# A list of 1371 steps in another order: linear-attention chunks, a weight fold and a multiplicative feed-forward block interleaved by one text

## The chip, the cores and the metric

The kernel runs on one core of one Trainium2 chip. Five engines work at once: TensorE (PE; its weight loads are listed apart as PEld), VectorE (DVE), ScalarE (ACT), GpSimd (POOL) and SyncE (SP), which here only issues transfers. The metric is the time of one execution in microseconds (us). The kernel before took 601.12 us, the median of three executions (600.37 to 601.99). A profile of one execution shows every instruction with its start, its length and what it waited for.

## The reference

Four batches of eight heads run a delta-rule recurrence over 768 positions with a head size of 48; the result, as 3072 tokens of 384 features, goes through a feed-forward block whose two input products are multiplied with each other.

```python
def _attn_ref(q, k, v, beta):                      # (4, 8, 768, 48), beta (4, 8, 768)
    k_n = k / (np.linalg.norm(k, axis=-1, keepdims=True) + 1e-06)
    state = np.zeros((B, H, D, D), dtype=np.float32)
    for t in range(S):
        kt, vt, bt = (k_n[:, :, t], v[:, :, t], beta[:, :, t, None])
        y[:, :, t] = np.einsum('bhd,bhde->bhe', q[:, :, t], state)
        v_old = np.einsum('bhde,bhd->bhe', state, kt)
        state = state + bt[:, :, :, None] * np.einsum('bhd,bhe->bhde', kt, vt - v_old)

def _moe_ref(x, w1, w2, w3, w_out):                # (3072, 384), 384x1024, 1024x1024, 1024x384
    a = x @ w1
    b = x @ w2
    h = a * b @ w3
    return h @ w_out
```

## The kernel before

The sequence is cut into 12 chunks m of 64 positions. Within a chunk the recurrence is a triangular system; two chunks together make one pair j (or u) of 128 positions, for which the triangular blocks are inverted at once. The weights w3 and w_out are multiplied into one 1024x384 matrix first (the fold), so that the feed-forward block needs two products with w1 and w2, their product element by element, and one more product. The last one is done with seven block products instead of eight, so sums of weight blocks and of activation blocks are formed on POOL. All weights are rounded on the way in: every 128-row piece goes through a raw buffer and is converted by two ACT passes (L717, L720), one DVE pass (L722) and one POOL pass (L724).

All of this is written as generators. A part is one generator, named by a letter and numbers; each time its name stands in ORDER, `step` runs it up to its next `yield`. So a step is the piece between two yields, mostly a few instructions of one engine. Below, X.n is the n-th time that X stands in the list, hence its n-th piece. After the list is through, `in_text_order` (L161) chains all instructions of each engine in the order in which they were written. Every engine, SP and ACT with their transfers among them, therefore executes in the order of the list and waits at the head of its own sequence; the list cannot change what is computed, only who comes first.

The parts, with the lines of their instructions:

- `k`m, `q`m, `v`m: load a chunk of k (L204, four transfers), q or v (L215, two). `k0` and `q0` are issued by ACT, all others by SP. `beta` loads and transposes beta (L961, L968, L973). `p`m loads a chunk in permuted form (L232, eight transfers for k, eight for q).
- `K`m, `Q`m (m below 4): transposes on TensorE (L339), copied out of PSUM by DVE and ACT (L351, L349). For the later chunks `d`m does this on DVE (L326).
- `g`j: squares on POOL (L272), row sums on DVE (L274), an exchange through TensorE (L257). `N`j: fifteen small DVE instructions for the norms (L281 to L305) and another exchange.
- `s`m: scores on TensorE (L369, L375), then DVE and ACT or POOL (L381, L393, L395, L399). `u`m stores the blocks to DRAM (L416).
- `V`j: loads the blocks (L428), inverts them with 31 pairs of DVE instructions (L442, L449) and stores them (L457). For the first two pairs, V0 and V1, the block lies in one of the two PSUM tiles of the kind `w`, which is held from the copies V.3 and V.4 (L436) to V.67 and V.68 (L453); until then the other parts that need such a tile share the one that is left.
- `e`m: loads the inverse (L466, L473), a DVE transpose (L485), two groups of small TensorE products (L502) with ACT copies (L518, L529) for the corner block.
- `n`m: v times the norm on POOL (L541). `c`m: the chain through the state, three groups of TensorE products of 64 passes or more (L555; c.1, c.3, c.5) with DVE after each (L588, L598, L617 or L619). `y`m: the outputs (L656, two groups with a drain between), ACT copies (L677), transfers within SBUF (L688).
- `P`i: loads a weight piece (L708): P0 to P3 w_out, P4 to P11 w3, P12 to P14 w1, P15 to P17 w2. `C`i: converts one half of a piece; piece i has C2i and C2i+1. There are three raw buffers, taken in turn, so a load waits for POOL to finish both halves of the piece three loads before.
- `t`i: transposes of w3 (L762, L765). `f`jc: the fold, two halves of four products with 384 columns (L771), then ACT (L778). f.1 needs C0 to C3, f.2 needs C4 to C7.
- `b`jc: chunk 0 of pair 0, and `a`ujc: the rest of pair u, in eight column blocks jc: product with w1 (L791), ACT copy (L803), product with w2 (L791), DVE multiplication (L807). Their PSUM tiles are four of the kind `f`, taken in turn.
- `T`: sums of weight blocks on POOL (L840). `S`u: sixteen sums of activation blocks on POOL (L860). `o`u: the seven block products (L888). `x`u: results on ACT and DVE (L919, L923, L925) and stores (L905).

TensorE's order therefore mixes long steps (a, b, o, f: four to sixteen products of 192 to 512 columns) with small ones (hundreds of matmul passes with 16 to 128 columns). The critical sequence at the start is: k and q in, K and Q, N0, s0 and s1, u0 and u1, V0, e0, c0, y0, c1, y1, and from there the products a and b. The fold and the transposes fill TensorE meanwhile.

Of the kernel before, what the change touches and what calls it, by code (L numbers as in the profile page):

```python
# [1064 lines left out]
```

## Time and profile before

| what | us |
|---|---|
| median of three executions | 601.12 |
| the profiled execution | 601.93 |
| its span, first to last instruction | 600.2 |
| TensorE busy | 542.4 |
| DVE / POOL / ACT busy | 329.7 / 173.6 / 164.2 |
| TensorE idle in 0 to 160 / 160 to 380 / 380 to 600 | 44.6 / 5.5 / 7.5 |
| mean granted TensorE clock, as a share of full speed | 0.98 |

Over the whole span TensorE is busy nine tenths of the time and no other engine more than 55%. In 40 slices (each digit the busy share of 15 us in tenths, 9 for 90% or more) the beginning differs from the rest:

```profile
PE   2378994889899999999999899999999999999997
DVE  2457763457786379665696644975545963211012
ACT  3486653734312211131211312012310111320100
POOL 6364433230535700207203016021071001500051
PEclk9988996899999999999999989999999999999999
DMA  8959887596953356525546352463253021010001
```

The DMA row is the mean busy share of the 16 transfer engines; it is high in the first eleven slices, in which all weights and the first chunks come in. The chain of waits, followed back from the last instruction, spends its time so:

```profile
PE 80%; DMA 6%; issue 4%; DVE 4%; ACT 4%; SPq 1%; POOL 0%; ACTq 0%; DVEq 0%
```

"issue" is time in which an engine waited for nothing that the profile shows. TensorE's own waits, longest in total first:

```profile
PE ps_f L339 <- DMA ktok<-in_k_dram: 11.0, 2, 9.2
PE ps_f L968 <- ACT KQ L349: 8.8, 1, 8.8
PE ps_w L502 <- issue: 7.8, 2, 6.1
PE ps_w L656 <- issue: 5.3, 5, 2.2
PE ps_w L375 <- issue: 4.7, 3, 2.2
PE ps_f L771 <- ACT w3T L765: 3.5, 2, 2.2
PE ps_f L791 <- POOL w2s L724: 2.8, 2, 2.3
```

A line names the engine, the tile and line that waited, what ended the wait, and then the sum in us, the number of waits and the longest.

### The profile page before, as it was taken

What the parts mean: (1) busy time and instruction counts of PE and PEld (TensorE: products, weight loads), DVE (VectorE), ACT (ScalarE), POOL (GpSimd) and SP (SyncE); (2) the same over time, 40 slices, a digit from 0 to 9 for tenths busy, and PEclk for the clock granted to TensorE, in tenths of its full rate; (3) what the DMA queues carried; (4) which work ended last, traced back from release to release, by engine and by line L of the source; (5) the groups of instructions that cost most, each with busy time, mean ns of one, the idle gap of its engine ahead of it and who ended that gap; (6) DMA issues with size and microseconds to landing.
All of it is one profiled execution on the core that took longest, in us unless ns stands there. A gap on an engine that the chain in (4) does not pass through costs nothing.

```text
span 600.2 us, 19394 instructions
## 1 busy us (share of the span) xinstructions
PE 542.4 (90%) x8444; PEld 378.7 (63%) x8444; DVE 329.7 (55%) x788; ACT 164.2 (27%) x345; POOL 173.6 (29%) x222
## 2 busy tenths in 40 slices
PE   2378994889899999999999899999999999999997
PEld 2364663658678884558854569645588446884477
DVE  2457763457786379665696644975545963211012
ACT  3486653734312211131211312012310111320100
POOL 6364433230535700207203016021071001500051
PEclk9988996899999999999999989999999999999999
DMA  8959887596953356525546352463253021010001
GB/s 225 219 135 276 233 163 128 82 176 96 164 80 55 56 123 108 98 42 84 103 78 127 50 81 73 82 114 65 40 86 94 14 59 32 5 54 13 1 0 53
DMA packets 204404, 56.54 MB, mean 94 GB/s; under 512 B 193344, under 2 KB 199488, under 8 KB 202528
## 3 DMA queue, kind: packets, MB, share of 16 engines
q1 hardware_dynamic: 200128, 54.52, 46.4%
q10 hardware_dynamic: 4192, 0.79, 0.9%
q8 instruction: 66, 1.08, 0.8%
q14 instruction: 18, 0.15, 0.1%
HBM read 43.09 MB, written 11.01 MB: 90 GB/s over the span
## 4 chain that ended last, share of the span: by engine, by line
PE 80%; DMA 6%; issue 4%; DVE 4%; ACT 4%; SPq 1%; POOL 0%; ACTq 0%; DVEq 0%
PE ps_f L791 39%; PE ps_f L888 18%; PE ps_w L555 5%; PE ps_f L771 5%; PE ps_w L656 4%; DMA raw<-in_moe_w_dram 3%; PE ps_w L502 3%; PE ps_w L369 2%; PE ps_w L375 2%; DMA ktok<-in_k_dram 2%; DVE ps_w L449 1%; DVE tb L442 1%; DMA Vd<-Vb 1%; ACT raw L720 1%; PE ps_w L888 1%
## 5 line engine op out<-in xcount | busy, mean ns | idle before, releaser
L791 PE MATMUL ps_f<-xT,w2s 128*128 128x512 f32 (+1 forms) x336 | 134.2, 544 | 3.0 <-POOL w2s L724 2.8
L860 POOL TENSOR_TENSOR ab<-ab 128x256 f32<-128x256 f32 x96 | 66.8, 728 | 223.5 <-DVE ab L807 190.0
L791 PE MATMUL ps_f<-xT,w1s 128*128 128x512 f32 (+1 forms) x336 | 128.2, 532 | 0.3 <-issue 0.3
L791 PEld LDWEIGHTS ps_f<-xT,w2s 128*128 128x128 f32 x336 | 62.5, 191 | 57.9 <-issue 50.9
L791 PEld LDWEIGHTS ps_f<-xT,w1s 128*128 128x128 f32 x336 | 63.3, 190 | 55.8 <-issue 51.7
L803 ACT COPY ab<-ps_f 128x512 f32<-128x512 f32 (+1 forms) x56 | 27.9, 527 | 185.6 <-PE ps_f L791 185.6
L888 PE MATMUL ps_f<-w,ab 128*128 128x192 f32 x376 | 66.3, 330 | 0.0
L807 DVE TENSOR_TENSOR ab<-ab,ps_f 128x512 f32<-128x512 f32 (+1 forms) x56 | 32.9, 604 | 59.1 <-PE ps_f L791 58.5
L888 PEld LDWEIGHTS ps_f<-w,ab 128*128 128x128 f32 x376 | 61.2, 190 | 3.9 <-issue 2.7
L442 DVE TENSOR_TENSOR tb<-Vb,Ub 128x31 f32<-128x31 f32 (+15 forms) x124 | 43.9, 354 | 16.4 <-DMA Ub<-Ud 13.0
L771 PE MATMUL ps_f<-w2s,w3T 128*128 128x384 f32 x128 | 45.4, 507 | 4.9 <-ACT w3T L765 3.5
L888 PE MATMUL ps_f<-room,ab 128*128 128x192 f32 x272 | 48.0, 330 | 0.8 <-DVE room L919 0.8
L449 DVE TENSOR_TENSOR Vb<-Vb,tb 128x31 f32<-128x31 f32 (+15 forms) x124 | 44.6, 360 | 4.3
L888 PEld LDWEIGHTS ps_f<-room,ab 128*128 128x128 f32 x272 | 44.1, 190 | 1.6 <-issue 1.1
L677 ACT COPY xT<-ps_w 48x256 f32<-48x256 f32 x96 | 30.5, 366 | 49.1 <-PE ps_w L656 48.6
L272 POOL TENSOR_TENSOR sq<-ktok 128x384 f32<-128x384 f32 x24 | 20.2, 852 | 75.7 <-DVE tb L442 39.1
L381 DVE TENSOR_TENSOR U<-ps_w,wt 128x512 f32<-128x512 f32 x24 | 16.5, 689 | 42.6 <-PE ps_w L375 42.5
L771 PEld LDWEIGHTS ps_f<-w2s,w3T 128*128 128x128 f32 x128 | 24.2, 195 | 21.5 <-ACT w3T L765 4.0
L375 PE MATMUL ps_w<-KQ 48*64 48x64 f32 x768 | 29.4, 227 | 6.3 <-issue 4.7
L724 POOL TENSOR_TENSOR w<-w,raw 128x512 uint32<-128x512 uint32 x16 | 20.7, 1298 | 33.1 <-DVE w L722 15.7
L375 PEld LDWEIGHTS ps_w<-KQ 48*64 48x64 f32 x768 | 26.1, 140 | 5.6 <-issue 3.9
L541 POOL TENSOR_TENSOR vtok<-vtok,n 128x384 f32<-128x384 f32 x24 | 19.8, 838 | 33.3 <-DMA vtok<-in_v_dram 33.3
(104 smaller groups left out, 644.7 us busy)
## 6 DMA issues: line engine op xcount, KB each, us to landing
raw<-in_moe_w_dram SPq DMA_DIRECT2D x8, 1024.0 KB, 8.1
vtok<-in_v_dram SPq DMA_DIRECT2D x24, 192.0 KB, 4.5
raw<-in_moe_w_dram SPq DMA_DIRECT2D x12, 384.0 KB, 6.7
out_dram<-osb SPq DMA_DIRECT2D x46, 96.0 KB, 2.7
ktok<-in_k_dram SPq DMA_DIRECT2D x44, 96.0 KB, 3.5
raw<-in_moe_w_out_dram SPq DMA_DIRECT2D x4, 768.0 KB, 5.0
Ud<-U SPq DMA_DIRECT2D x48, 64.0 KB, 2.3
Ub<-Ud SPq DMA_DIRECT2D x6, 512.0 KB, 3.9
```

The source lines that it names most:

```text
L375: pe.matmul(ps[half(z ^ j), 1, n + C * j : n + C * j + C], lhsT=x[:, 0, :], rhs=x[:, j, :], start=True, stop=True,)
L442: dve.tensor_tensor(out=tv, in0=V[:, 0 : s + 1, s : s + 1].to_broadcast([P, s + 1, n]), in1=U[:, s, s + 1 : BS].unsqueeze(1).to_broadcast( ...
L449: dve.tensor_tensor(out=o, in0=o, in1=tv, op=ALU.subtract)
L555: pe.matmul(out(ps, r, h, z), lhsT=lhs(r, h, z), rhs=rhs(r, h, z), start=True, stop=True,)
L656: i = pe.matmul(region(h, z, r), lhsT=lhs, rhs=rhs, start=part[n] not in part[:n], stop=part[n] not in part[n + 1 :],)
L677: act.copy(out=xT[f, p:NP:2, b : b + NR, cc, :].rearrange("p a r t -> p r a t"), in_=pyv[f, z, b : b + NR],)
L771: pe.matmul(ps[:, 0:DM], lhsT=w3Ts[jc, kc // 4][:, kc % 4 * P : kc % 4 * P + P], rhs=wo[:, kc], start=(kc == 0), stop=(kc == KF - 1),)
L791: pe.matmul(ps[:].rearrange("p b c t -> p b (c t)"), lhsT=w[:, m, js], rhs=x[:, m, :, c0:c1].rearrange("p b c t -> p b (c t)"), start=(m = ...
L803: act.copy(out=t, in_=ps)
L807: dve.tensor_tensor(out=t, in0=t, in1=ps, op=ALU.mult)
L860: pool.tensor_tensor(out=o_, in0=x_, in1=y_, op=op)
L888: pe.matmul(ps[b][:, b, :], lhsT=abs_[u, HF * f + i][:, t0 : t0 + P], rhs=ws_[w][:, i], start=first and i == 0 and (b == 0 or n == "F"), s ...
```

## The change

ORDER is replaced by another list with the same 1371 entries: each name stands in it as often as before, so every step is run once and issues the same instructions. No instruction, tile or transfer is added or removed; all that changes is the order on each engine and in the two transfer queues, and with it which buffer of a group taken in turn a step gets. The new list was laid out by a planner that puts all transfers in one line, and the packets in which TensorE's instructions are fetched in that line too. The list is all that the diff holds. Cut to its beginning, up to the first products with w2 and a little beyond, and its end:

```diff
--- before.py
+++ after.py
@@ -37,53 +37,54 @@
 ORDER = """
-k0 K0 P0 C1 P5 C0 C0 C10 C11 k1 q0 C10 K1 V0 C11 P6 C12 g0 C13 g0 g0 g0 g0 C1 K0 K0 C10 C1 g0
-beta beta C0 K1 K1 g0 K0 K1 g0 K1 K0 C12 g0 g0 beta N0 Q0 Q0 Q0 Q0 Q0 q1 Q1 Q1 N0 C11 C13 C12
-Q1 P4 s0 N0 C13 Q1 C9 s0 s0 s0 s0 t2 t2 k2 C9 C9 C8 s0 Q1 s0 t3 t3 P1 g1 s1 C8 C8 s1 s1 s1 s1
-s1 g1 g1 t5 P9 C3 C3 C2 t1 t5 C18 K2 C2 C19 C18 C18 t1 K2 C3 K2 u0 u1 P2 C2 C19 g1 C19 K2 t0 K2
-V0 V0 t4 t0 f0 V0 C4 C4 C5 t4 C5 t10 V0 V0 V0 P3 P8 V0 V0 V0 V0 C5 C6 V0 V0 V0 C6 C7 V0 f1 C17
-V0 V0 V0 s1 V0 V0 f2 q2 t10 C7 C4 V0 C6 V0 V0 V0 V0 V0 V0 V0 V0 C16 C16 V0 V0 C7 f0 f1 f2 V0 V0
-V0 C16 C17 k3 f1 g1 f0 V0 V0 V0 t11 V0 V0 f2 V0 t11 t8 P7 t8 V0 C15 C15 P10 V0 V0 C14 V0 V0 Q2
-Q2 v0 f5 f4 C17 V0 V0 C21 f5 V0 V0 Q2 Q2 V0 Q2 t9 g1 V0 C14 V0 V0 V0 g1 C20 V0 V0 V0 V0 C15 f5
-V0 P11 C14 V0 C22 V0 V0 V0 t6 V0 t9 n0 V0 V0 v1 f4 g1 V0 n0 V0 f4 P13 t6 C20 s2 C23 g1 s0 C22
-g1 C22 C20 t7 V0 t7 C21 f3 N1 f3 f3 C21 q3 t12 t12 t13 t14 t13 e0 e0 C27 K3 K3 e0 t14 s2 s2 Q3
-C23 e0 Q3 e0 s2 Q3 e0 c0 K3 K3 e1 e1 s2 Q3 s2 K3 e1 e1 C23 t15 Q3 c0 y0 C27 s3 s3 s3 V1 y0 C26
-C26 f6 N1 s1 n1 N1 s3 s3 C27 s3 c0 P12 C26 f6 P14 u2 C24 e1 C24 C29 C24 c0 n1 c1 C28 C25 C28
-C28 t15 f6 u3 c1 P15 e1 f7 V1 V1 C25 C25 C29 c1 C30 c1 C30 f7 V1 V1 V1 V1 V1 C29 V1 y1 y1 C30
-f7 V1 V1 y0 b2 C31 b2 b5 V1 V1 P17 b3 V1 V1 V1 V1 V1 V1 V1 b5 b4 V1 V1 V1 c1 b6 V1 b6 y1 a05 b3
-V1 V1 C31 V1 V1 C31 V1 b4 a01 a01 V1 V1 V1 a00 V1 V1 a05 a00 V1 V1 V1 C34 P16 V1 a06 b0 b7 a06
-V1 b0 V1 V1 V1 V1 C32 C33 b7 p4 b1 V1 V1 V1 V1 C32 a07 V1 V1 a07 C34 a04 V1 V1 V1 V1 a04 V1 V1
-V1 V1 V1 V1 V1 V1 V1 a02 V1 V1 k4 g2 V1 V1 b1 a03 d4 d4 a03 C32 C34 a00 b0 C33 C35 a02 a00 v3
-k5 b1 n3 C35 b0 b1 a03 a03 g2 g2 b2 b2 g2 a01 C35 V1 b3 v2 c1 a01 C33 b3 b6 a07 n2 V1 b6 V1 g2
-g2 p4 a06 g2 c2 g2 g2 d4 d4 e2 e2 e2 a04 e2 n2 a07 c2 a06 e2 s4 e2 T b4 g2 N2 s4 c2 s4 T a02 c2
-c2 c2 y2 b4 p5 y2 b5 d5 s4 a04 e3 S0 V2 d5 a05 a02 o0 T N2 e3 n3 c3 a05 s4 s4 b5 T c3 S0 e3 p5
-d5 d5 b7 b7 u4 e3 S0 S0 S0 S0 e3 s5 S0 k6 N2 x0 o0 S0 s5 e3 s5 s5 s5 u5 s5 c3 g3 o0 g3 c3 x0 y3
...
-n10 e11 a40 c10 a43 a44 a45 e10 a44 c10 e10 e10 e11 e10 a42 a42 c10 o4 a44 S4 S4 S4 c10 e11 x4
-S4 S4 c10 S4 e11 o4 S4 e11 c10 c11 S4 o4 c11 e11 c11 S4 c11 S4 y10 S4 y10 S4 y11 S4 x4 S4 o4 o4
-y11 x4 x4 o4 x4 x4 y11 x4 a50 x4 x4 a50 S4 S4 o4 x4 a50 a55 a55 a50 a55 a51 a57 a51 a55 a51 a51
-a54 a54 a56 a57 a52 a52 a52 a53 a56 a53 a56 a53 a52 a54 a57 a54 x4 a56 S5 S5 S5 a53 o5 a57 o5
-S5 S5 x5 o5 x5 S5 S5 S5 S5 S5 o5 o5 S5 S5 x5 o5 S5 x5 S5 x5 S5 S5 o5 x5 x5 x5 x5 x5 x5 x5 x5 x5
+k0 g0 g0 g0 beta beta k1 g0 g0 K0 K0 beta K0 V0 K0 K0 P0 C0 C1 C0 C0 P6 C1 P5 q0 C13 g0 g0 C10
+g0 C10 C12 K1 C13 K1 C12 C1 K1 P4 C10 K1 g0 g0 K1 C11 C13 q1 Q0 Q0 Q0 t2 Q0 Q0 C12 s0 P9 Q1 C8
+N0 s0 C9 C11 C11 C9 C9 t2 Q1 Q1 N0 k2 N0 Q1 C8 C8 t4 Q1 C18 s0 t5 s1 s1 C19 C18 s1 C19 C19 s1
+t4 P1 P2 C18 s0 s0 t1 s0 C2 C2 C2 u0 s1 s1 t1 t5 u1 C4 P3 t0 g1 s1 t0 t3 C5 C3 C3 s0 V0 K2 K2
+t3 K2 C3 f2 C4 C4 K2 C7 C7 K2 f0 C5 C5 P8 C7 V0 V0 V0 V0 V0 V0 P7 C6 C6 V0 V0 f1 V0 V0 V0 V0 V0
+V0 V0 V0 C6 V0 P11 C17 f2 f2 V0 V0 f0 V0 V0 V0 C16 C16 q3 f0 t10 C16 t11 C17 s0 C17 f1 C15 f1
+t8 t10 q2 t9 P10 f5 V0 V0 V0 V0 V0 V0 V0 V0 V0 V0 V0 V0 C15 V0 V0 V0 t8 C14 C14 V0 V0 V0 V0 V0
+C15 V0 V0 V0 V0 t11 Q2 C22 f5 C14 V0 V0 V0 V0 V0 k3 Q2 V0 V0 V0 V0 V0 V0 V0 V0 V0 V0 V0 Q2 Q2
+Q2 s2 V0 C21 t9 f5 t6 t6 v0 n0 V0 K3 V0 g1 V0 C22 n0 g1 K3 K3 t7 C23 C23 P13 V0 v1 g1 g1 f4 f4
+f4 C22 g1 C23 C21 f3 C20 K3 K3 g1 g1 e0 g1 g1 t7 P14 e0 Q3 Q3 C26 e1 C27 e0 N1 f3 C20 Q3 s2 f3
+s2 s2 C21 e0 C26 e0 e0 s2 u2 V1 t13 t14 t14 C28 t13 Q3 s2 Q3 c0 e1 C20 t12 t12 e1 c0 y0 y0 e1
+P12 f6 C27 C27 s3 s3 C25 y0 s3 s3 s3 u3 C24 C29 s3 f6 f6 c0 v2 C28 C25 s1 e1 t15 e1 c0 n1 n1 c1
+t15 c1 V1 V1 V1 V1 V1 V1 V1 V1 V1 C29 C28 C26 C24 n2 V1 f7 V1 f7 V1 V1 V1 V1 V1 V1 V1 V1 c1 c1
+V1 V1 V1 V1 V1 V1 V1 V1 V1 V1 V1 V1 V1 C29 C25 b5 b7 f7 b7 V1 V1 V1 P17 N1 N1 V1 V1 V1 V1 V1 V1
+V1 V1 V1 V1 V1 y1 b5 b6 b4 y1 c1 C35 C34 b4 b6 C34 P15 V1 V1 V1 C24 b0 b3 C31 C30 k4 C30 c1 V1
+V1 b0 y1 b3 b1 a04 a06 a04 V1 V1 V1 V1 V1 V1 V1 V1 C34 a06 P16 g2 g2 b1 C30 C33 C33 C33 b2 V1
+g2 b2 C32 a07 a07 a01 C32 a00 p4 C32 d4 a01 n2 d4 V1 V1 C35 c2 a03 a00 v3 a05 a03 C35 a05 a02
+V1 C31 C31 V1 V1 V1 b2 a01 a04 V1 a01 b2 a02 n3 p4 d4 a03 b3 V1 k5 a04 a02 a07 e2 b3 c2 n3 a03
+T T a02 e2 g2 a07 a06 e3 e2 e2 d4 b7 a06 g2 e2 g2 g2 b1 e2 g2 g2 c2 e3 g2 c2 b5 b7 b5 b1 c2 y2
+b0 a00 p5 b4 y2 c2 d5 d5 v4 e3 s4 N2 e3 b6 b0 a00 V2 s4 s4 e3 c3 e3 p5 d5 b4 S0 a05 s4 c3 d5 s5
+s4 T s5 k6 a05 o0 x0 T b6 S0 N2 u4 s5 S0 S0 S0 s4 S0 s5 s5 u5 c3 c3 s5 V2 v5 o0 y3 y3 V2 V2 y3
+N2 S0 S0 o0 n4 n4 S0 S0 x0 x0 o0 V2 V2 p6 S0 V2 o0 x0 c3 V2 V2 V2 V2 V2 S0 o0 x0 x0 x0 x0 V2 V2
...
+V5 V5 V5 V5 V5 V5 V5 V5 V5 V5 V5 V5 V5 a40 a44 a44 V5 a46 e10 a46 a43 a43 c9 a40 a47 e10 a47
+a41 a40 a41 x3 N5 e11 c10 c10 e10 e10 a45 a40 N5 a45 S4 S4 e10 o4 n11 e10 S4 c10 e11 e11 e11
+c10 o4 c10 x4 o4 y10 x4 S4 S4 S4 c10 y10 S4 n11 S4 o4 e11 e11 c11 x4 S4 o4 c11 c11 c11 S4 S4 S4
+S4 S4 y11 x4 y11 S4 S4 y11 o4 x4 x4 x4 o4 x4 x4 a54 x4 a54 a54 a52 a52 a54 a51 a51 a51 a56 a55
+a51 a57 a57 a56 a57 a55 a57 a56 a50 a50 a56 a50 a53 a53 a53 a50 a52 a53 a52 a55 a55 o5 S5 S5 S5
+S5 S5 S5 o5 S5 S5 S5 S5 S5 S5 x4 x5 o5 S5 x5 o5 o5 o5 S5 S5 x5 x5 x5 x5 S5 o5 x5 x5 x5 x5 x5 x5
+x5 x5
 """
```

On TensorE the order of the first steps was K0.1, K1.1, beta.2, g0.9, Q0.1, Q1.1, N0.2, s0.1, s0.5 and is beta.2, K0.1, K1.1, g0.9, Q0.1, t2.1, s0.1, Q1.1, N0.2. On SP the loads were P0, P5, k1, P6, beta, q1, P4, k2, P1, P9, then u0, u1, P2; they are beta, k1, P0, P6, P5, P4, q1, P9, k2, P1, P2, then u0, u1. From o5.1 on TensorE's order is the same.

## The prediction

> **What bounds the kernel now.** I read the shares of the engines first, then busy time by stage, then the chain of waits in order of time. Columns of the stage rows: stretch, its length, busy time and instructions of each engine, granted TensorE clock, DMA share, GB/s.
>
> ```profile
> PE 542.4 (90%) x8444; PEld 378.7 (63%) x8444; DVE 329.7 (55%) x788; ACT 164.2 (27%) x345; POOL 173.6 (29%) x222
> q8 instruction: 66, 1.08, 0.8%
> ```
> ```profile
> 0.00:50.00 50.00, 23.37 (x561) 20.12 (x562) 20.29 (x53) 29.39 (x54) 28.43 (x41) 0.94 0.88 209
> 50.00:78.00 28.00, 26.71 (x155) 16.59 (x154) 23.64 (x70) 17.48 (x34) 13.30 (x13) 0.98 0.91 233
> 78.00:100.00 22.00, 18.00 (x519) 14.00 (x517) 11.79 (x31) 11.05 (x21) 8.14 (x8) 0.90 0.74 132
> 100.00:133.00 33.00, 23.46 (x590) 16.47 (x591) 12.06 (x29) 14.82 (x31) 9.80 (x8) 0.86 0.79 133
> 133.00:160.00 27.00, 23.83 (x168) 19.84 (x167) 22.07 (x58) 14.39 (x37) 5.52 (x5) 1.00 0.78 120
> 160.00:380.00 220.00, 214.46 (x3893) 153.85 (x3892) 144.31 (x342) 41.10 (x94) 66.53 (x90) 0.99 0.47 84
> 380.00:600.00 220.00, 212.54 (x2567) 137.84 (x2565) 95.55 (x210) 35.93 (x78) 41.93 (x59) 1.00 0.23 48
> ```
> ```profile
> 77.20 1.08 ACT Vb L453 x2
> 78.31 6.14 DMA Vd<-Vb
> ...
> 99.45 6.15 issue
> ...
> 128.68 2.22 issue
> ...
> 156.56 2.54 POOL w2s L724 x2
> ...
> 223.50 25.75 PE ps_f L791 x60
> ...
> 250.91 2.77 PE ps_f L791 x6
> ```
>
> TensorE is busy for 542.4 of 600.2 us, and no TensorE work goes away. From 160 us on it is idle for 5.5 and 7.5 us of two stretches of 220. So time can come from the 44.6 us that it is idle before 160 us, from a clock below 1.00 there, and from the spacing of its steps afterwards. Of the 44.6, 26.6 lie in the first 50 us (loads and conversions), 16.6 between 78 and 133, 3.2 after. Between 78 and 133 two things alternate: the serial chain that starts when the first block inverse V0 ends on DVE at 77.2 (copy, write of Vd, e0, c0, y0, c1, y1, the first products), and gaps called "issue", in which TensorE waited for nothing the profile shows. The largest, 6.15 us, lies inside e1.3. Over 94 to 106 us the DMA view holds a single packet of queue q8, over 60 to 90 us two; the page counts 66 of them for 16,888 weight loads and matmuls, 256 a packet. I read these gaps as waits for TensorE's own instructions behind full transfer queues.
>
> **The change, step by step.** I followed the new list on each engine from the start, with each step at its duration in this trace and each transfer at the time between landings here (a k or q load 3.0 us, an early weight load of 1 MB 3.4, of 768 KB 2.4), and took the later of engine, queue and operand. All clock times below that are not of the trace are estimates from such rows.
>
> *Start to the end of V0: 0, bounds -3 and +9.* On SP beta and k1 go ahead of the weights, so K0 can start at 8.6 (9.16 now). On ACT C10.1 needs P5, now the third weight load (about 22 us), and it stands ahead of Q0.2 to Q0.5; these end at 29 (30.1 now). P9 and k2 go ahead of P1: P9 waits on SP until C12.3 and C13.3 free its raw buffer (27.4), so P1 issues at 33 instead of 24.06. Behind P1 come C2.1, C2.2 and s1.6. I get s1.6 at 40.5 (39.7 now) and u1 issued by 42.6 (42.4 now), so Ub lands at 49 as now. On ACT V0.3 moves behind C7.1, which needs P3: 50.2 instead of 46.0; V0's first DVE operation is at 50.5 (49.51 now). Inside V0 DVE no longer waits 2.56 us for C15.2 nor does a g1 reduction of 0.55, but it waits about 1 for C16.2. V0 ends at 77. The upper bound is P1's whole 9 us, if nothing hides it; the lower is the stall and reduction removed. I take 0, since the intermediate times, but for V0.3's, agree with now's within 1.1 us. The folds f0 to f5 cover this, as now; without them TensorE would idle with V0.
>
> *V0 to c0: 1.0 gained.* The write of Vd took 6.14 us, with P13 (issued at 74.07) ahead of it in the queue; its median on the page is 2.8. P13 now goes about 5 us earlier, so the write gains 3.3. But N1.1, 15 DVE instructions from 81.6 to 86.2, moves from before e0.2 to after it and ahead of s2.2, and on ACT f3.3 stands ahead of e0.4. s2.4 waits for the bank that s2.2 and s2.3 empty, until 92.3; behind it in TensorE's order are e0.5 and c0.1. c0.1 starts at 95.5 (96.5 now).
>
> *The packet gaps: 7.9 gained, bounds 0 and 7.9.* Counting neighbours in TensorE's order, the run of small steps t12.1 to s3.1 now has 560 matmul passes and no long step in it. In the new list f3.2, f6.1 and f6.2 (2.8 us each) cut it into 316 and 196. If the 6.15 us and the slow clock around it are gone, y0.1 ends at 100 instead of 108.9: 8.9 ahead with the 1.0 before. The old run's gaps were 1.04, 2.19, 6.15 and 0.26, or 1.7 us per 100 passes. At that density the new 316 passes would still lose 5.4; at the best, nothing. I put half, 2.7, into the sum.
>
> *c0 to the first products: 2.6 gained.* c1.3 ends at 118.6 (125.1 now), but with f7.2 already done: 9.3 ahead. y1.1 took 4.8 us with a gap of 2.22 in it; after two products it should take 2.2 to 2.4. It ends at 124 (132.6 now), with b5.1 and b7.1 (1.45 each) done: 11.5 ahead.
>
> *First use of w2: 2.2 gained.* The sixteen products with w1 end at 155.6, and TensorE waits to 159.1 for C32.3 and C34.3 on POOL, which stood behind g2.1. P16 moves ahead of p4 as now but is issued at 130, not 140; C34.3 passes g2.1 and C32.3 is done at 142.5, before TensorE needs it at 146.5 with c2.1 also done: 12.6 plus 1.1 is 13.7 ahead.
>
> *Steady part: 1.2 gained, bounds -4 and +5.* Ten products in a row take 25.75 us, 2.575 each; a product followed by a small step takes 2.77, and the way back costs about 0.1 (a c.1 step 1.08 against 0.97). The new list goes from long to small steps 51 times instead of 46: 5 times 0.3 is 1.5 lost. Runs of over 250 small passes fall from two to none (gaps of 1.61 and 0.75, and after the first a clock of 0.83 over 10 us, 1.7): 4.1 gained. Runs of 192 rise from three to six, with gaps of 0.74, 0 and 0.58 now: 3 times 0.44 is 1.3 lost. Net 1.2. Stores and perm loads change places on SP (x2.11 goes behind e8 and e9, p10.1 ahead of u8); TensorE's other work covers these, and if it does not, one such issue costs up to 4 us. The final steps, from the first o5 on, have the same order on TensorE: nothing.
>
> Sum: 13.7 - 2.7 + 1.2 = 12.2 gained on the profiled execution's 601.93 (span 600.2 and 1.73 around it): 589.7. The median of the three runs, 601.12, lies 0.81 below that execution; 588.9 would be its equal. I say **590.0**, as I walked only the first 160 us instruction by instruction.
>
> Two rules of the Trainium skill speak against parts of this. "Runtime: NRT & Kernel Launch", section "Instruction fetch mechanics", says that an engine's instructions come in 16 KiB blocks of 256, which the trace's 1.08 MB in 66 packets bears out, and that fetching them is mostly hidden; by it the gaps are no packet waits (a rival below). The single packet in 12 us speaks against "hidden" here. "TensorE: Matmul & The Clock Gate", section "What's actually happening", says that an idle window of about 3.4 us halves the clock; the walk leaves TensorE idle from 88.7 to 92.3, so by the rule 1.7 us more, 591.7. The trace agrees in kind: 0.54 was granted over 95 to 110 us.
>
> **The rivals.**
> *The packets stay where the load is.* P14 (four transfers, 1 MB) now goes ahead of e1's loads and P12 behind u2, so the stretch from 92 to 104 is still full of transfers, and shorter runs may not help. For it: DMA share 0.74 and 0.79 there. Against it: f6.1 right behind y0.1 gives a packet 2.8 us. Then the old run's 9.6 us of gaps come back where I set 2.7 aside: 12.2 less 6.9 is 5.3, 597.
>
> *The gaps are no packet waits.* Then TensorE's sequencer waits in them for something that the list does not move, the 7.9 is not gained and the 2.7 not needed: 589.7 + 7.9 - 2.7, 595. For it: the profile names no releaser. Against it: the packet of 102.48 took 1.60 us, so landed at 104.1, 1.5 before TensorE went on at 105.59.
>
> *Slower: V0 slips.* The three raw buffers form a ring: each weight load on SP waits for POOL to finish the load three before. V0.3 stands behind C7.1, so behind P3, P9 and P6, two turns of the ring, each with two ACT passes of 1.1, a DVE pass of 0.45 and two POOL passes of 1.3 behind other work. P6 to P9 took 20.2 us now, P9 to P8, which follows it in its buffer, 15.9. If each turn comes 7 us later than I walked it, V0 starts at 64.5 and all behind it follows, as the folds end before: 590 + 14 = 604. It decides from 62 on for V0's first DVE operation, where the gain is gone. For it: ACT already stalls 10.11 us in the first 21 for one weight load. Against it: the walked times.
>
> *No change:* c1 and the first products wait for w1 and w2 anyway, since all weights must pass the same queue (DMA share 0.88 in the first 50 us): 601. Against it: the queue had 0.74 to 0.79 after 78.
>
> *More:* no gap is left in the new runs and TensorE is full from 95: the 2.7 come back and the steady part reaches its bound, 583. That the list does not do what it says I exclude: each engine is chained in the list's order.
>
> **How the numbers follow.** Forecast 0.42 (own range 584 to 596), packets stay 0.16, no packet waits 0.05, slower 0.22, no change 0.08, more 0.07. This kernel's measurement can tell 0.3%, 1.8 us, from no change. Faster: 0.42 + 0.07 + 0.05 + 0.13 of the packets' 0.16 = 0.67; same 0.08 + 0.03 = 0.11; slower 0.22. The range runs from 580, the middle of the case of more, to 606, a V0 that slips by 16; about 0.15 lies outside.
>
> **What would show it.** Right: V0's first DVE operation at 48 to 53; no issue gap over 3 us between 90 and 110; y1.1 done before 127; no wait for POOL at the first product with w2; TensorE's idle time before 160 us near 32. Wrong: V0 after 55 points to the ring, a gap of 5 us or more to the packets; a stage after 160 us with over 4 us more idle, to the steady part, of which I know least.

## The result, and the profile after

The new list is slower: 608.81 us, the median of four executions (607.67 to 610.09), against 600.75 (597.73 to 601.99); the ratio is 1.0142 (95% interval 1.0098 to 1.0186). The profiled execution took 609.29, its span is 607.5. On another chip, beside the experiments below, the ratio was 1.0139 (1.0097 to 1.0181). An execution that lies more than 1.5% above the fastest of its kernel counts as slow, and the ratios here and below leave such executions out.

From the page of the kernel after: engine totals, the packets of instructions, the chain that ended last.

```profile
PE 551.8 (91%) x8444; PEld 382.3 (63%) x8444; DVE 343.1 (56%) x788; ACT 166.2 (27%) x345; POOL 176.8 (29%) x222
...
q8 instruction: 66, 1.08, 0.8%
...
PE 57%; DVE 18%; DMA 11%; issue 4%; SPq 4%; ACT 4%; POOL 1%; DVEq 0%; POOLq 0%; ACTq 0%
```

The instructions are the same in number, but TensorE is busy 9.4 us longer and DVE 13.4 us longer, and DVE's share of the chain went from 4% to 18%. The same stages of the kernel after, with the columns of the prediction:

```profile
0.00:50.00 50.00, 30.55 (x582) 23.76 (x583) 24.84 (x57) 32.81 (x60) 31.46 (x43) 1.00 0.90 235
50.00:78.00 28.00, 26.25 (x262) 16.85 (x261) 24.80 (x67) 18.17 (x33) 12.64 (x12) 1.00 1.01 230
78.00:100.00 22.00, 16.86 (x468) 11.92 (x466) 12.18 (x31) 14.71 (x31) 8.90 (x10) 0.92 0.70 110
100.00:133.00 33.00, 24.99 (x578) 18.40 (x582) 22.14 (x56) 15.46 (x34) 7.19 (x6) 0.93 0.92 146
133.00:160.00 27.00, 27.00 (x206) 23.18 (x199) 15.22 (x38) 7.71 (x19) 16.06 (x15) 0.90 0.77 126
160.00:380.00 220.00, 209.64 (x3789) 148.26 (x3788) 143.42 (x319) 41.30 (x94) 57.61 (x78) 0.98 0.45 79
380.00:600.00 220.00, 213.00 (x2562) 136.79 (x2561) 97.89 (x218) 36.03 (x78) 42.95 (x60) 1.00 0.21 44
```

Before 160 us TensorE is now idle for 34.4 us (44.6 before). From 160 to 380 it is idle for 10.4 (5.5 before), at a clock of 0.98. TensorE's waits after 200 us, the kernel after first and the kernel before second:

```profile
PE ps_w L556 <- DVE S L620: 3.1, 2, 2.5
PE ps_w L503 <- DVE T L486: 3.0, 2, 2.6
PE ps_f L792 <- DVE ab L808: 1.4, 1, 1.4
PE ps_f L889 <- DVE osb L920: 1.3, 1, 1.3
```
```profile
PE ps_w L656 <- issue: 2.3, 3, 1.0
PE ps_w L502 <- issue: 1.6, 1, 1.6
PE ps_f L888 <- DVE room L919: 0.8, 1, 0.8
```

Before, TensorE hardly waited for DVE there. Now four sorts of DVE result are late: the corner block's T of e, the state S of c, the products ab, and the results osb that empty a bank. To size this, I take the time from the end of y3.1 to the end of o5.7 on TensorE, and split it into idle time, half the busy time at a granted clock of 0.5, and the rest:

| kernel | end of y3.1 at | y3.1 to o5.7 | idle | lost to half clock | rest |
|---|---|---|---|---|---|
| before | 209.3 | 386.9 | 5.9 | 1.7 | 379.3 |
| after | 199.0 | 404.4 | 15.0 | 5.0 | 384.4 |
| after, second profile | 200.6 | 401.6 | 12.7 | 5.1 | 383.8 |

The start is ahead by 10.3 us in this pair of profiles, and 17.5 are lost behind it. The lead differs from profile to profile, and is sized below.

The largest wait behind a batch of DVE work is the one in front of c6.1. First some DVE instructions of the kernel after in order of time (start, length, line, tiles with partitions x elements), then POOL's over the same time:

```profile
200.09 0.19 DVE L443 TENSOR_TENSOR tb<-Vb,Ub 128x31 f32<-128x31 f32 x1 [5.27 <-DMA Ub<-Ud]
...
283.73 0.67 DVE L443 TENSOR_TENSOR tb<-Vb,Ub 128x31 f32<-128x31 f32 x1
...
289.37 0.71 DVE L443 TENSOR_TENSOR tb<-Vb,Ub 128x135 f32<-128x135 f32 x1
290.11 0.30 DVE L450 TENSOR_TENSOR Vb<-Vb,tb 128x135 f32<-128x135 f32 x1
...
292.30 0.87 DVE L450 TENSOR_TENSOR Vb<-Vb,tb 128x192 f32<-128x192 f32 x1
...
295.29 0.40 DVE L450 TENSOR_TENSOR Vb<-Vb,tb 128x231 f32<-128x231 f32 x1
295.61 1.93 DVE L620 TENSOR_TENSOR S<-S,ps_w 48x768 f32<-48x768 f32 x2
```
```profile
277.94 2.79 POOL L861 TENSOR_TENSOR ab<-ab 128x256 f32<-128x256 f32 x4 [15.23 <-DVE ab L808]
280.68 1.62 POOL L273 TENSOR_TENSOR sq<-ktok 128x384 f32<-128x384 f32 x2
282.25 7.66 POOL L861 TENSOR_TENSOR ab<-ab 128x256 f32<-128x256 f32 x11
291.99 0.96 POOL L542 TENSOR_TENSOR vtok<-vtok,n 128x384 f32<-128x384 f32 x1 [2.08 <-DVE Vb L450]
```

Two things come together. **The place in the list:** V3.3 to V3.13, twenty-two DVE instructions, stand ahead of c5.6, the state update; the old list has c5.6 ahead of V3.3. c5.5 ended at 291.41 on TensorE, but S was made from 295.61 on, and c6.1 waited. **The length:** the same instruction of 31 elements takes 0.19 us at 200.09 and 0.67 at 283.73, and the change back to 0.30 at 290.11 comes as POOL ends its sums at 289.9; one more long one (0.87 at 292.30) lies beside POOL's L542. All 62 DVE instructions of V3 take 27.6 us here, 21.2 before; those of V2 take 25.0 against 22.2. The twenty-two take 11.2 here and 6.8 before. An estimate from these: at 6.8 they would have ended 4.4 us earlier, at 291.3, just as c5.5 ended, so at this place the length decides as much as the place in the list.

In front of e4.3 the late result is DVE's too, but there DVE was not busy. Its transpose of T waited for a transfer; the two transfers ahead of it, the line of DVE, and the instruction queue in the DMA view from 237.3 to 242 us:

```profile
237.38 4.49 DMA Vd<-Vb
...
242.78 2.29 DMA TT<-Vd
```
```profile
245.16 0.71 DVE L486 STREAM_TRANSPOSE T<-TT 128x512 f32<-128x512 f32 x1 [3.70 <-DMA TT<-Vd]
```
```profile
q8 instruction: 1, 0.02, 2.2%
```

DVE stood idle for 3.70 us until the inverse of pair 2, written to Vd from 237.38 on, had landed and was read back. One packet of TensorE's instructions began 0.7 us into that write, which took 4.49 us. In the eight profiles of new lists in which such a packet began within 1.8 us of this write's start (after, twice, m1 to m4, q1 and t2 below) the write took 3.88 to 4.77 us; in seven others without one (before, s1, m6, t1, t1b, p1 and p2) 2.61 to 2.63; in s2, where one began 2.4 us in, 2.91. Where e4.3 follows a13.3 as here, its wait goes with it: 2.06 us behind a write of 3.88, 3.04 behind one of 4.77. That the packet delays the write is argued from this agreement; no run moved the packet alone.

After such a wait the clock goes down: half clock was granted for 6.8 us from 247.8 on (behind a wait of 2.62 at e4.3) and for 3.4 us from 299.0 on (behind 2.49 and 0.58 at c6.1).

### The profile page after: what moved, and what is told of

The parts are those of the page before. It is cut to its first block, busy times and chain, and to the rows that moved or that the text cites. A ratio compares the mean times of both kernels' runs of the same rounds, so it can differ in the third digit from the quotient of the medians.

```text
span 607.5 us, 19397 instructions
## 1 busy us (share of the span) xinstructions
PE 551.8 (91%) x8444; PEld 382.3 (63%) x8444; DVE 343.1 (56%) x788; ACT 166.2 (27%) x345; POOL 176.8 (29%) x222
## 4 chain that ended last, share of the span: by engine, by line
PE 57%; DVE 18%; DMA 11%; issue 4%; SPq 4%; ACT 4%; POOL 1%; DVEq 0%; POOLq 0%; ACTq 0%
PE ps_f L792 28%; PE ps_f L889 13%; DVE tb L443 6%; DVE Vb L450 6%; PE ps_w L556 4%; PE ps_w L657 4%; PE ps_f L772 2%; PE ps_w L503 2%; DMA Vd<-Vb 2%; DMA TT<-Vd 2%; DMA raw<-in_moe_w_dram 2%; PE ps_w L370 1%; SPq L233 1%; DMA xT<-xT 1%; PE ps_w L376 1%
## 5 line engine op out<-in xcount | busy, mean ns | idle before, releaser
L792 PE MATMUL ps_f<-xT,w1s 128*128 128x512 f32 (+1 forms) x336 | 130.8, 543 | 1.8 <-DVE osb L920 1.3
L443 DVE TENSOR_TENSOR tb<-Vb,Ub 128x31 f32<-128x31 f32 (+15 forms) x124 | 47.8, 386 | 11.0 <-DMA Ub<-Ud 7.5
L450 DVE TENSOR_TENSOR Vb<-Vb,tb 128x31 f32<-128x31 f32 (+15 forms) x124 | 49.7, 401 | 4.3
L889 PE MATMUL ps_f<-room,ab 128*128 128x192 f32 x272 | 49.9, 338 | 0.0
L273 POOL TENSOR_TENSOR sq<-ktok 128x384 f32<-128x384 f32 x24 | 21.1, 885 | 95.9 <-PE ps_w L556 30.0
L889 PEld LDWEIGHTS ps_f<-room,ab 128*128 128x128 f32 x272 | 45.7, 196 | 0.7
L542 POOL TENSOR_TENSOR vtok<-vtok,n 128x384 f32<-128x384 f32 x24 | 21.1, 891 | 52.0 <-DMA vtok<-in_v_dram 34.2
L519 ACT COPY T<-ps_w 32x512 f32<-32x512 f32 x24 | 13.8, 576 | 75.6 <-PE ps_w L503 46.9
L370 PE MATMUL ps_w<-KQ 48*64 48x128 f32 x384 | 28.3, 281 | 5.6 <-DVE PT L400 2.1
L327 DVE STREAM_TRANSPOSE KQ<-perm 128x512 f32<-128x512 f32 x32 | 21.4, 692 | 17.8 <-PE ps_w L657 8.4
```

The costliest lines, as they stand in the source:

```text
L370: pe.matmul(ps[half(z), 0, n : n + 128], lhsT=x[:, 0, :], rhs=x.rearrange("p j t -> p (j t)"), start=True, stop=True,)
L443: dve.tensor_tensor(out=tv, in0=V[:, 0 : s + 1, s : s + 1].to_broadcast([P, s + 1, n]), in1=U[:, s, s + 1 : BS].unsqueeze(1).to_broadcast( ...
L450: dve.tensor_tensor(out=o, in0=o, in1=tv, op=ALU.subtract)
L792: pe.matmul(ps[:].rearrange("p b c t -> p b (c t)"), lhsT=w[:, m, js], rhs=x[:, m, :, c0:c1].rearrange("p b c t -> p b (c t)"), start=(m = ...
L889: pe.matmul(ps[b][:, b, :], lhsT=abs_[u, HF * f + i][:, t0 : t0 + P], rhs=ws_[w][:, i], start=first and i == 0 and (b == 0 or n == "F"), s ...
```

## The experiments

All kernels hold the same 1371 steps; only the list differs. "Stretch" below is the time from the end of y3.1 to the end of o5.7.

**Two splices: which part wins, which loses.** In s1 the new list is followed up to y3.1 (616 steps) and the remaining steps stand in the old list's order; s2 is the reverse.

```diff
-<new list>
+<new list up to y3.1>  <all other steps, in the old list's order>      (s1)
+<old list up to y3.1>  <all other steps, in the new list's order>      (s2)
```

> The new list up to y3.1 (TensorE at 199 us), then all other steps in the old list's order. Theory A (the new start is worth about 7 us of TensorE work, and the loss sits in the steady part, in places where the new list makes TensorE wait for DVE): 593 to 596, 0.987 of before, no wait over 1.5 us between 200 and 300. Rival B (the lead is worth nothing, since the chain of block inverses on DVE sets the pace after 200 us whatever the order): 599 to 602, a new wait at e4 near 243. Rival C (the loss is spread over many switches between long and small steps): as A.

> The old list up to y3.1 (TensorE at 209 us), then all other steps in the new list's order. Theory A: the old start and the new steady part's loss of 14, so 612 to 616, with a wait of over 2 us at e4.3 and another at c6.1. Rival B (the lead ran into the DVE chain): without the lead DVE keeps up, 601 to 604. Rival C: 612 to 616 with no single wait over 2 us.

s1: 594.55 us, 0.9876 of before (0.9829 to 0.9924); y3.1 ended at 200.0, the stretch took 388.3: idle 6.4, no half clock, rest 381.9. s2: 620.89, the median of three executions, 1.0298 (1.0231 to 1.0366); the stretch 406.3. So the start is a real gain and the rest a real loss, as theory A has it; rival B falls, since the lead was kept to the end in s1. s2 is 5 us above A's range: at its seam o0 waits 5.58 us for a sum of DVE, and the wait at c6.1 (2.48) stands as in the new list, while that at e4.3 is gone (0.35 is left, at e4.5).

Set against s1, the new list's stretch is 16.1 us longer: 8.6 of idle time, 5.0 of half clock, 2.5 of the rest. Rival C, for which s1 and s2 say the same as A, is held to about these 2.5, since switches show in the rest. V2's 62 DVE instructions take 25.2 us in s1, as long as in the new list, and nothing waits for them there.

**Single moves.** m1 moves V3.9 to V3.13 behind c5.6, m2 moves a product ahead of e4.3.

```diff
-V3.7 V3.8 V3.9 V3.10 o1.4 p8.1 V3.11 V3.12 c5.5 o1.5 x1.3 V3.13 v7.1 c5.6 c6.1 x1.4
+V3.7 V3.8 o1.4 p8.1 c5.5 o1.5 x1.3 v7.1 c5.6 V3.9 V3.10 V3.11 V3.12 V3.13 c6.1 x1.4      (m1)
-e4.3 d6.4 s6.1 N3.1 s6.2 s6.3 e4.4 e4.5 e4.6 a13.4 a11.3
+a11.3 e4.3 d6.4 s6.1 N3.1 s6.2 s6.3 e4.4 e4.5 e4.6 a13.4                                 (m2)
```

> The new list with one move: V3.9 to V3.13 go behind c5.6, so DVE makes the state update of c5 after V3.8 and not after V3.13; TensorE's order is unchanged. Theory A: the wait of c6.1 (2.49 and 0.58 us) and the 3.4 us of half clock after it go, 4.8 us: 604, and V3 ends 1 to 2 us later, which nothing feels. Rival C (such a wait only moves on to the next small step): 607 to 609.

> The new list with one move: the product a11.3 goes ahead of e4.3 on TensorE. Theory A: the wait of e4.3 (2.62 us) is filled by the product, a wait of at most 0.7 stays at e4.5 or c4.3, and the 6.8 us of half clock after it go, together 5 to 6 us: 603. Rival C: the wait moves behind the product, 607 to 609. Half a theory (the wait goes, but the clock is halved there anyway): 606.

m1: 1.0124 (1.0055 to 1.0194), stretch 402.5. m2: 1.0149 (1.0083 to 1.0215), stretch 405.8. Both expectations of theory A failed. TensorE's waits from 235 to 320 us, m1 and then m2:

```profile
PE ps_w L503 <- DVE T L486: 3.0, 1, 3.0
PE ps_f L889 <- DVE room L920: 3.0, 1, 3.0
```
```profile
PE ps_w L556 <- DVE S L620: 3.1, 2, 2.5
PE ps_w L556 <- DVE PT L400: 2.6, 1, 2.6
```

In m1 the wait for S is gone, but o1.6 waits as long for the sum into room (x1.4), which still stood behind V3.13. In m2 the wait for T fell to 0.6, but c4.3 waits 2.6 for a bank that s6 empties on DVE behind the fifteen instructions of N3.1. In both the wait goes on to the next step that needs DVE, as rival C said; the times are above its 607 to 609.

**Moving all that stands behind the batch.** In m3 the V steps go behind x1.4 too; m4 adds, at e4, s6.1, N3.1, s6.2 and s6.3 behind c4.4.

```diff
-V3.9 V3.10 o1.4 p8.1 V3.11 V3.12 c5.5 o1.5 x1.3 V3.13 v7.1 c5.6 c6.1 x1.4
+o1.4 p8.1 c5.5 o1.5 x1.3 v7.1 c5.6 c6.1 x1.4 V3.9 V3.10 V3.11 V3.12 V3.13      (m3 and m4)
-e4.3 d6.4 s6.1 N3.1 s6.2 s6.3 e4.4 e4.5 e4.6 ... a11.3 ... c4.3 c4.4
+a11.3 e4.3 d6.4 e4.4 e4.5 e4.6 ... c4.3 c4.4 s6.1 N3.1 s6.2 s6.3               (m4)
```

> The new list with V3.9 to V3.13 behind x1.4, so that DVE makes both the state update c5.6 and the sum into room x1.4 before it goes on with V3; TensorE's order is unchanged. Theory A, made sharper (after 200 us TensorE waits for whatever DVE step stands behind a batch of V steps; moving one of them only exposes the next): now neither c6.1 nor o1.6 waits, no wait over 1 us and no half clock between 288 and 300; 4.6 to 4.8 us less than the new list, 1.006 of before. Rival D (these waits are the price of a TensorE that is ahead of DVE; one that goes comes back at the next small step whatever the order): 1.012 to 1.014, with a wait of 2 to 3 us at another DVE result before 340.

> As the run before, and at e4: the product a11.3 ahead of e4.3, and s6.1, N3.1 (15 DVE instructions), s6.2, s6.3 behind c4.4, so that no bank of the kind w waits for N3. Theory A: the wait of 2.6 to 3.0 us at 243 and the 6.8 us of half clock go, about 1.5 of short waits for ACT copies stay: 5 us less than the run before, 0.997 to 0.999 of before. Rival D: the wait comes back behind c4.3, 1.006 or more.

m3: 603.33, 1.0059 (1.0025 to 1.0093), as theory A says; the stretch is 399.0, 5.4 shorter than the new list's, and no wait over 0.3 us is left between 273 and 303. m4: 1.0056 (1.0019 to 1.0093), stretch 398.3: the 5 us expected of e4 did not come. Its waits from 235 to 320 us:

```profile
PE ps_w L503 <- ACT T L519: 1.1, 2, 0.7
PE ps_w L556 <- ACT TT L530: 0.9, 2, 0.7
```

Short waits for ACT copies (0.71, 0.35 and 0.68 us within 249.8 to 252.5) are all that is left at e4, yet 6.8 us of half clock begin at 251.9, as long as in the new list. So removing the long wait alone does not remove the half clock there; what causes it stays open.

**The cause put into the old list.** In i1 the old list gets V3.3 to V3.13 ahead of c5.6, and nothing else; TensorE's order is the old one.

```diff
-c5.6 V3.3 V3.4 ... V3.5 ... V3.6 ... x1.4 ... V3.12 x1.6 ... V3.13
+V3.3 V3.4 V3.5 V3.6 V3.7 V3.8 V3.9 V3.10 V3.11 V3.12 V3.13 c5.6 ... x1.4 ... x1.6
```

> The old list with the suspected cause alone put in: V3.3 to V3.13 go ahead of c5.6 on DVE, as in the new list; TensorE, ACT, POOL and SP keep the old order. Theory A: c6.1 waits some 5 us for S near 294, half clock follows for 3.4 to 6.8 us: 7 to 9 us more than before, 1.012 to 1.015. Rival D: TensorE without the lead does not feel it, under 2 us, 1.000 to 1.003.

```profile
PE ps_w L555 <- DVE S L619: 6.3, 2, 5.8
```

These two, 5.81 and 0.45 us, are the only waits from 270 to 320 us, where the old list has none, and 6.8 us of half clock begin at 289.3. The stretch took 393.5, 6.6 more than with the old list (idle 11.6 against 5.9). So a batch ahead of c5.6 makes TensorE wait, as theory A says. It is not the same wait as in the new list, though:

```profile
281.66 0.19 DVE L442 TENSOR_TENSOR tb<-Vb,Ub 128x31 f32<-128x31 f32 x1 [6.69 <-DMA Ub<-Ud]
```

V3.3 had to wait for its own load, with c5.6 behind it, and began 2.6 us after the end of c5.5 (279.02); in the new list it began 7.7 ahead of it. No POOL work lies beside V3 here, and its 62 instructions take 21.2 us. The time does not show the loss: of four executions one took 598.97, below the median of before (600.57), and the others 610.2 to 613.8, too far apart to compare.

**POOL beside DVE.** q1 is m3 with V3.3 to V3.8 behind x1.4 too.

```diff
-V3.3 V3.4 V3.5 V3.6 x1.2 y5.1 y5.2 V3.7 V3.8 o1.4 ... c5.6 c6.1 x1.4 V3.9
+x1.2 y5.1 y5.2 o1.4 ... c5.6 c6.1 x1.4 V3.3 V3.4 V3.5 V3.6 V3.7 V3.8 V3.9
```

> The run m3 with V3.3 to V3.8 moved too, so that all of V3's DVE work stands behind c5.6 and x1.4, by which time POOL has finished the sums S1. Theory S (an instruction of V2 to V5 on DVE takes about twice as long while POOL works on an elementwise instruction of its own): the 62 instructions of V3 take 21 to 22 us, not the 27.1 of m3, and though V3 starts some 7 us later than in m3 it ends at most 3 us later. Rival R (the long ones come of something in V3 itself, or of the list's place of V3 among transfers): they take 26 to 28 us and V3 ends 7 us later. The time: 1.003 to 1.008 of before either way, as nothing waits for V3's end but e6.

V3's 62 instructions took 22.9 us, not 27.1; V3 started 12.4 us later than in m3 and ended 5.2 later. Theory S said 21 to 22, and at most 3 later. Most of the stretching (4.2 of the 5.9 us over the 21.2 of an unstretched V3) went with POOL's sums. The remaining 1.7 lies on the four instructions from 312.26 to 315.78 (0.63 and three of 0.93, where the next takes 0.42), beside POOL's L273 and L542 from 311.78 to 315.50. So theory S holds for all of it; its 21 to 22 missed because POOL had other work there too. The time, though, was 1.0199 (1.0148 to 1.0250): o1.7 waited 2.88 us for a result osb, which now stood behind eleven pairs of V3. The expectation "nothing waits for V3" was right of its end, and wrong of what it stands ahead of.

**DVE itself, at e4.** m6 is m3 with the four row sums of g3 taken out of V2, long steps between e4.3, e4.5 and c4.3, s6 and N3 behind, and a37.4 on DVE ahead of V4.28.

```diff
-g3.1 g3.2 ... g3.8 ... V2.34 ... e4.2 e4.3 ... s6.1 N3.1 s6.2 s6.3 e4.4 e4.5 ... a11.3 ... c4.3 c4.4 a16.1
+g3.1 ... V2.34 ... e4.2 g3.2 g3.3 g3.4 g3.5 e4.3 a11.3 ... e4.4 e4.5 ... g3.6 g3.7 g3.8 ... a16.1 c4.3 c4.4 g3.9 g3.10 s6.1 N3.1 s6.2 s6.3
```

> The run m3, and at e4 the fix on the side of DVE: the row sums g3.2 to g3.8 (four on DVE, with their squares on POOL) out of V2 and behind e4.2, so that V2 ends 3 to 5 us earlier; on TensorE e4.3, a11.3, e4.5, a16.1, c4.3, then g3.9 and s6.1 with N3 behind; and a37.4 on DVE behind V4.27 and not V4.33 (a34.3 waited 1.37 us for it). Theory A: no wait over 1 us between 235 and 260 nor at 407, no half clock at 248; from the end of y3.1 to the end of o5.7 392 us (404.4 with the new list, 399.0 in m3, 386.9 with the old list), 0.993 to 0.998 of before. Rival D: the waits come back at other DVE results, 398 or more for that stretch and 1.004 or more.

```profile
PE ps_w L657 <- DVE PT L400: 4.3, 1, 4.3
```

1.0136 (1.0085 to 1.0187), stretch 400.8. From its first to its last DVE instruction V2 took 34.1 us, 2.5 less than in m3; the write of its inverse took 2.63, without a packet in it. The waits at e4.3 and at 407 are gone, but y4.1 waits 4.3 us for the bank that s6 empties once N3 is through, and e8.3 waits 1.79 at 415. Time and stretch are rival D's. That DVE has too much work there is not shown: from the end of e4.2 to the end of s6.3 it was idle for 6.0 of 15.3 us, half of that at c4.4 in a wait for TensorE, and only then came N3 and s6.

**One stretch of the list.** t1 takes the old order for y3.1 to o1.6 alone, t2 the new order there and the old behind it.

```diff
+<new list up to y3.1>  <old order up to o1.6>  <new order>      (t1)
+<new list up to o1.6>  <old order>                             (t2)
```

> The new list to y3.1, then the old list's order to o1.6 (TensorE at 291 in the splice s1), then the new list's order for all the rest. Theory E (nearly all of the loss lies in the one stretch between y3.1 and o1.6, in the order of that stretch, which took 104.2 us with the new list and 91.3 in the splice; the rest took 300.3 and 297.0): y3.1 to the end of o5.7 in 391 to 393 us, 0.991 to 0.995 of before. Rival F (the new list's later part loses by itself, and the stretch only takes part of it): over 397, 1.002 or more.

> The new list up to o1.6, then the old list's order. Theory E: y3.1 to the end of o5.7 in 400 to 402 us, 1.007 to 1.011 of before, so the whole loss of the stretch and none of the rest's. Rival F: under 396, 1.001 or less.

t2: 1.0104 (1.0067 to 1.0140), stretch 401.3, as theory E says; y3.1 to o1.6 took 104.3, the rest 297.1. t1: 1.0118 (1.0077 to 1.0158), stretch 401.6, both rival F's; y3.1 to o1.6 took 91.1, as in s1, but at the seam a24.1 waited 6.66 us. t1b moves the steps that it waited for:

```diff
-o1.6 N3.2 N3.3 V3.12 V3.13 v7.1 S1.16 x1.5 x1.6 ... x1.10
+o1.6 v7.1 S1.16 x1.5 x1.6 V3.12 V3.13 ... x1.10 N3.2 N3.3
```

> The run t1 with its seam mended: there N3.2 (left over from the stretch) took the bank of the kind f that a24.1 takes in the new list, so a24.1 waited 6.66 us for x1.8 behind V3.14 to V3.16, and 3.4 us of half clock followed. N3.2 and N3.3 now go behind x1.10, V3.12 and V3.13 behind x1.6. Theory E: no wait over 1 us near 290; y3.1 to the end of o5.7 in 391 to 393 us, 0.991 to 0.996 of before. Rival F: over 397, 1.002 or more.

0.9998 (0.9965 to 1.0032), between E and F; the stretch, 398.1, is rival F's. y3.1 to o1.6 took 91.3; of the 306.8 behind it, 2.7 are waits still at the seam, and two spells of half clock lost 3.4. So y3.1 to o1.6 costs the new list 11 to 13 us (102.3 to 104.3 in three profiles against 91.1 to 91.3 in four), which is shown, and its later part 2 to 4 (299.3 and 300.3 against 296.1 to 297.1); the seam keeps t1b from showing how much more of it is really its own.

**Packets.** In s1 a wait of 3.49 us lay inside c1.5 at 130.8, with a packet of instructions that landed at 132.8. p1 moves the loads of k4 behind y1's transfers, p2 behind the weight load P16 as well (steps of SP alone).

```diff
-k4.1 ... y1.3 P16.1 p4.1
+... y1.3 k4.1 P16.1 p4.1      (p1)
+... y1.3 P16.1 k4.1 p4.1      (p2)
```

> The spliced list (new up to y3.1, then old) with one move on SP: the four loads of k4 (96 KB each) go behind the six transfers of y1. TensorE's order is unchanged. Theory P (the wait of 3.49 us inside c1.5 is a wait for a packet of TensorE's instructions behind full transfer queues): the packet starts some 4 us earlier, the wait falls below 1.5 us and the 6.8 us of half clock after it go, 3 to 6 us less than the splice, 0.978 to 0.983 of before, if k4, ten us later, holds nothing up. Rival Q (the wait is TensorE's sequencer's own): the wait stays at 3 to 4 us, 0.987. If k4 is late then: a new wait at c2 or e2 between 145 and 175.

> The splice again, with the loads of k4 behind y1 and behind the weight load P16, so that w2 is not late (in the run before, P16 went behind k4 and a03.1 waited 3.36 us for ACT, which stood at a conversion of P16). Theory P: no wait over 1.5 us inside c1.5 and none over 1 at 147; 3 to 6 us less than the splice, 589 to 592, 0.980 to 0.983 of before. Rival Q (packets come late again elsewhere, the sum over 100 to 160 stays): 0.987.

TensorE's waits from 100 to 160 us, of s1, p1 and p2 in turn, each the one inside c1.5 and, where the move made one, the longest new one:

```profile
PE ps_w L556 <- issue: 3.5, 1, 3.5
```
```profile
PE ps_f L792 <- ACT ab L804: 3.4, 1, 3.4
...
PE ps_w L556 <- issue: 0.3, 1, 0.3
```
```profile
PE ps_f L792 <- POOL w2s L725: 2.2, 1, 2.2
...
PE ps_w L556 <- issue: 0.6, 1, 0.6
```

The wait inside c1.5 fell from 3.5 to 0.3 and 0.6 without a change of TensorE's order, and it ended 1.4 to 1.5 us after the packet had landed in all three (132.8 and 134.31; 131.9 and 133.32; 131.0 and 132.53). So it is a wait for the packet, as theory P says. That moving k4 cured it is shown only in part: the packet began at 131.3, 130.4 and 129.4, so 0.9 and 1.9 us earlier and not 4, and TensorE came to this place at 130.8, 133.0 and 131.9, so 2.2 and 1.1 later. When a packet is asked for, no run shows. The time did not follow: 0.9932 (0.9899 to 0.9966) and 0.9931 (0.9899 to 0.9963), since other waits took its place (for ACT at 147, for w2 at 151).

**The start, sized.**

> The splice s1 again (new up to y3.1, then old), on the same chip as the new list, to size the new start: the first time 0.9876 (0.9829 to 0.9924), two variants of it 0.993. Theory A: 0.984 to 0.991. If the start is worth less than the first run said: 0.991 to 0.995.

> The new list unchanged, beside the splices on one chip: 1.012 to 1.017 of before by what it took the first time; the splice should lie 0.022 to 0.028 below it.

On one chip the splice is at 0.9899 (0.9865 to 0.9933) and the new list at 1.0139 (1.0097 to 1.0181), 0.024 apart. The splice beats both lists; the new start is worth 6 to 8 us.

## Why the prediction was wrong

**The start was forecast right in kind, and too large: 11.0 against 6 to 8.** Its five signs came: V0's first DVE operation at 48.3; no issue gap over 3 us from 90 to 110 (2.36 is the longest); y1.1 done at 125.5 (but at 130.9 in the second profile); no wait for POOL at the first product with w2; 34.4 us idle before 160. The terms: *start to the end of V0: 0* looks too low, as V0 ended at 73.0 and at 77.2 before; but with the old start it ended at 72.9 in i1 and at 73.5 in s2, so 0 may well be right. *V0 to c0* and *the packet gaps*: y0.1 ended at 96.4, not 100. But the packets' loss, set at 2.7, was 2.36 at 106.2 and 3.96 at 128.7, and 3.4 and 6.8 us of half clock came after them; so b2.3 began at 153.0, not 146.5. The loss had been sized by the length of the runs of small steps, and the 3.96 came inside c1.5, 64 passes between two long steps. The 11.0 is the sum to there, 13.7 less 2.7; the 6 to 8 are the splice's. One reading of the rows was off: by them TensorE is idle for 13.5 us between 78 and 133, and for 1.3 between 50 and 78, not for 16.6.

That the gaps are packet waits was right. As in s1, p1 and p2, TensorE went on 1.4 to 1.5 us after the packet had landed before the change (104.1 and 105.59) and after it (131.2 and 132.63).

**The step that failed is the steady part: "1.2 gained, bounds -4 and +5".** It came out at 16.1 lost against s1 (14.3 for the second pair of profiles, 401.6 and 387.3). The term counted switches, packets and places on SP, all of them costs on TensorE or SP. What it counted came out near: the rest, in which switches show, grew by 2.5 (1.5 forecast), issue waits after 200 us fell from 3.9 to 2.2, and the 1.7 lost to half clock at 344.8 went (together 3.4; 4.1 less 1.3 forecast). It put waits for DVE at nothing, without a reason: "I walked only the first 160 us instruction by instruction". Both lists have long batches of V on DVE (up to 36 instructions in the old, 60 in the new); what differs is the step behind them. The old list has c5.6 ahead of V3.3, the new one has V3.3 to V3.13 ahead of c5.6, and that was to be read off the list. Moving that batch (m3) gave back 5.4 us of the stretch. At e4 the wait (2.62) and the half clock behind it (3.4 lost) are as large, and there DVE itself waited for a write that took 4.49 us; no run gave these back. "TensorE's other work covers these" was said of SP's transfers; it did not cover this one.

**Two prices were missing from the sum.** Behind waits of 2.1 to 3 us came 3.4 to 6.8 us of half clock, 1.7 to 3.4 lost: 5.0 of the 16.1. And V's instructions were taken at their length in the trace of before, where POOL was idle beside V3 (0.0 us; 11.5 after). The Trainium skill has this: "SBUF — State Buffer", section "Who interferes with whom", says that a DVE instruction with two inputs in SBUF contends with a GpSimd instruction that reads SBUF, and calls the port pair that they share an exclusive lock. The traces agree: V2 and V3, with both inputs in SBUF, are stretched from 0.19 to 0.67; V0 and V1, whose block lies in PSUM, take 21.4 and 21.3 us with 9.1 and 12.7 us of POOL beside them, as long as before.

**The rivals.** V0 did not slip; the slower result came from a part for which I had named no slower rival, only a bound of -4. The sign "a stage after 160 us with over 4 us more idle" is what happened (4.8 more from 160 to 380). The packets stayed in part (6.3 of the 9.6 us).

Open: which steps the later part's 2 to 4 us come from, what part of e4's loss is the packet's, and why the clock was halved there in m4 with short waits alone.

## What to carry to other kernels

When an order is changed, read each engine's sequence past the stage of interest: for every result that the busiest engine waits for, list what now stands ahead of it on the engine that makes it, and count those at the length they have beside the other engines' work. If that engine stood idle before the late result, look at what it waited for in turn: at e4.3 it was a transfer. A wait that goes when one step is moved comes back at the next step of the same engine, until the whole batch is behind them. A list that is better in one stage can be spliced with another from a step at which both have done nearly the same.

## What the runs showed of the hardware

- Half clock came for 3.4 us or a whole multiple of it (6.8, 10.2). Behind single waits of 2.1 to 6.7 us it began 1.8 to 5.3 us after the wait had (108.56 and 110.41 in p1, 241.14 and 246.37 in t2; the longest wait, 6.66 at 289.49 in t1, had it from 293.8 on). The length of one wait does not settle it: 3.4 us of half clock also came behind a wait of 0.96 (at 438.29, from 439.7 on, m4), while waits of 2.22 and 2.29 (128.68 and 155.61, before), 2.94 (131.40, t1b) and 1.3 to 1.4 (386.7, 411.4 and 539.9, after) were followed by none. The Trainium skill, "TensorE: Matmul & The Clock Gate", section "What's actually happening", asks for an idle window of about 3.4 us; here less was enough.
- A write of 512 KB took 3.9 to 4.8 us when a 16 KB packet of instructions began within its first 1.8 us, and 2.6 without one.
- The same DVE instruction, with both inputs in SBUF, takes 0.19 us alone and 0.67 beside POOL's elementwise work, so a small one loses most: its length becomes that of POOL's (0.70 each).
- The same order up to y3.1 ended at 209.3, 199.7 and 204.6 in three profiles (before, i1 and s2), with 20.5 us of half clock up to there in the first two alike: a difference of this size in the start needs several profiles.
